# Attention beside an MLP on one core: the main loop's order on five engines from one searched table, with shared PSUM places

## The chip, the core and the metric

The kernel runs on one core of a Trainium2 chip. The core has a matrix engine (PE, with its weight loads shown apart as PEld), a vector engine (DVE), an activation engine (ACT), a general engine (POOL) and an engine that issues most DMAs (SP). The metric is device time in microseconds (us), the median of several runs.

## What is computed

A layer norm of the input is fed to two branches, and all is summed: attention with 32 query heads of 16 columns that share one key and one value head, and a two-layer MLP with the Mish function.

```python
# B, S, D, H, Dh, F = 1, 2048, 512, 32, 16, 1792
xn = layernorm(x)                                   # over D, eps 1e-5
q  = (xn @ wq) as 32 heads of 16;  k, v = xn @ wk, xn @ wv    # [S, 16]
p  = softmax(q @ k.T * Dh ** -0.5)                  # per head, [S, S]
attention = concat(p @ v) @ wo
h   = xn @ w1 + b1
mlp = (h * tanh(softplus(h))) @ w2
out = x + attention + mlp                           # all in float32
```

## The kernel before

**Tiles.** Tokens are cut into 4 chunks `c` of 512; `X[c]` is the transposed, normed chunk as a high and a low part. Weights and activations are split in the same way (`split`: ACT copies the high part, POOL subtracts to get the low part), and a product of two is the sum of three terms. The 32 heads of 4 chunks make 32 units `u` of 4 heads and 512 queries each. A unit needs three passes:

- `s`: scores of queries (rows) against keys, 64 tiles, whose maxima DVE takes straight from PSUM (TENSOR_REDUCE into `nm`). At a unit's end the maxima are negated, transposed by PE (`mt`), split by DVE (`mhl`) and sent by four SP DMAs into rows of the unit's query tile `QS` (`place_maxima`).
- `e`: the scores again, transposed and with the maxima already subtracted, 64 tiles of 128 keys x 512 queries. ACT takes the exponential out of PSUM into a probability slot `pt`.
- `o`: value steps, 16 a unit, each four matmuls (one a head, 32 columns of the array each) that add into one PSUM tile; each shows twice in the trace (4096 rows for 2048 matmuls). ACT reads the tile out (`ov`) after the 16th.

Maxima of unit u+1 run beside exponentials and value steps of unit u. In between stand the products of the MLP and of the output projection, cut into pieces that fill one PSUM tile: `h` (X by w1, 56), `y` (activation by w2 in five parts, 80) and `f` (attention by wo, 12, and four at the very end). Mish goes through ACT (exponential, logarithm, exponential), DVE (a clamp, `tu`) and POOL.

**Lanes and value steps.** Contraction of `s` and `e` needs 64 rows or fewer, and products of 128 rows are cut into two halves. So PE works in lanes: a matmul of 64 rows on the upper half of the array beside another on the lower half. Two neighbours on different halves run at once, and I call that a slot of the lanes; where the next matmul is for the same half, one half stays empty for a slot. Value steps use all 128 rows, and between lanes and value steps PE changes its mode.

**PSUM and slots.** PSUM has eight tiles of 512 columns: three for `s` (`m`), one pair (`e2`) and one single (`e1`) for `e`, one for half products (`misc`), one for `o`. Probabilities lie in three pairs (`WIDE`) and four singles (`SINGLE`), ten heads in all. An exponential is wide (two heads, one ACT instruction of 1024 columns) or single.

**What sets the order.** `PLAN` is a string with one letter for each action: a value step, or a pair of jobs for the two lanes (maximum, wide, single, half or nothing), with or without a drain of PE ahead of it. `commit` carries an action out and lets a class `Clock` with prices for each operation tell when weights, Mish stages and maxima are due (`later`, `run_due`, `flush`). PE, ACT, DVE and POOL then work in the order in which the calls were made; the order of SP's DMAs was set by the framework. Blocks of w1, w2 and wo are split once, stored to DRAM (`w_dram`) and loaded again from there (`block`); `X` has two places, chunks 2 and 3 are stored ahead of the loop and loaded again (`need_x`).

Ahead of the loop stand loading, layer norm, transposes, keys, values, all queries (stored to `q_dram`) and the maxima of unit 0. Behind it stands `last_quotient`: the sum, division and projection of the last unit.

Of the kernel before, what the change touches and what calls it, by code (L numbers as in the profile page):

```python
# [31 lines left out]
FILLS = 3 * (2 * NC * DT * FT + 2 * NC * DT * DT - DT) - 3 * DT * DT  # L32
ACTS, RING, QTS = 7, 6, 3


SLOT, LOAD, DRAIN = 0.228, 0.105, 0.19
VALUES, INTO_VALUES, INTO_LANES = 0.87, 0.1, 0.13
READY, LATE, BACK = 0.43, 0.115, 0.165
REDUCE, EXP1, EXP2 = 0.598, 0.477, 0.904
ADD, POOL_ADD = 0.6, 1.3  # L40
STEP = 3.2
SLACK, OVERDUE = 0.5, 6.0
WEIGHTED = "wq", "w1", "w2", "wo"
WEIGHTS, FIRST = 8.0, 14.0
ATTENDED = 5
WIDE, SINGLE = 3, 4
U_MAX = 16384.0

# [5 lines left out]
JOBS = None, "maximum", "wide", "single", "half"  # L54
ACTIONS = ["values", "place"] + [(a, b, d) for a in JOBS for b in JOBS for d in (False, True)]
LETTERS = ".!" + string.ascii_letters
PLAN = (
    "ssRtisRtssiRQAQSQUQQyQUtwCq.Gww.qow.soo.qsCCsMsRyQUQ.myq.ssCsCsVQOQQSSGQ.myq.ssMsCCsM.myq.wwUQ.QQUSSQQOUQtCq"
    "Cs.mMCCs.sMssCs.qsCRUQQSSQ.GwQSOUQ.GwQS.QQQUSSQOG.QSotsMisCCsMs.qmy.qoCs.GwCRQUQSSQUQ.myG.ssiysMs.yssq.ysssM"
    "iisCCq.mwUS.QQUQOSQ.MsCssiMsiisCq.GQQSOOQUOQSQS.ssMsCCsiiG.ASQQQU.yUQQQ.GCCssisiiG.oAQQOOQOSQUo.Gmy.Mym.qQOQ"  # L60
    "SSG.QSSQtMssCCsMs.yq.sssMCCsiiq.RUQSSQQOOG.MCCssq.qSSQQOG.qym.MssCCsMRQSSQUQ.Gym.qyss.qCCssiq.qCCssiG.GSQSQO"
    "UQOQSQS..qCCssiMsiysMs.CAm.yQQQUOOQSSUQQ..sAsCsisMisy.mqy.QGSQSOQUOQ.GCCssiMsisy.wUw.QQUQyOQUQ.wGSQ.QUQyQOQU"
    ".tssMCCsisq.QQQSUSQOQNsCsCsM.oqo.Gsys.Gym.UQSSQQUQOOQuSG.osMo.MsCCss.qCCss.GQQSSOQOOUQOQy.qmy.MssysiMs.qCCss"
    "iG.QQUSSQQOUQOQy.qwo.MsssCCMs.ossAis.ymG.yQUQQOOSQUo.GssCCisMis.UyQQQ.GSQSQOG.qCCssiMsisy.QUQSSQQU..qwStsiMs"
    "isCCq..qCCssiMsisyq.wSGQ.QUSSQQQ.qsCCsiMsisysM.CAm.yQQQUOOQSSQUQ..oCssMisiCCsq.mAw.UQyQQOUQOOQSUw.qsCo.MssCC"
# [24 lines left out]
    "my.GQSQSOQOUQ.GCCssiMsisy.qmy.UwwQ.QUQSSQQg.CCsMssiisy.GwS.QUSSQQQU.wCMssisiCsA.myQU.QQQUSSQ.GoCsiiMsisCCsM."  # L90
    ".qwwOOOUQOQSSQUQ.mys.qCCssisMiCCsq.mAw.QQUQSSQOUQ.wSUm.oCssMisiCCsq.ssG.GQSSQOQUOQSQS.MssCCsM.mqy.MmCo.qwSQO"
    "OUQQSSG.sssCCMs.qoCs.Gwo.GSSQQOUQOyQG.myq.ymG.oAm.sssMCsCisMisRSQUQS.QQSUQS.sMssCCs.MCCssq.GSSQQOUQOQSSQ..qC"
    "CssiMsisCCq.msA.GQSQOOQUOQSQSG.qCCs.qCCssiG.GSSQQOUQOQSSQ.qmCC.MCmw.USSQQQU.GssCCis.qCsCsMsRSQSQ.Gym.USSQQQU"
    ".qssCCiMsisiis.Ao.GQQSSOG.ysssMiisCCq.mwS.QQUSSQQU.ssMCCssiMsisy.Gw.UQSQQOUQOyQUQ..qCsCsiMsisy.wUQQSOQOUQ.Ms"
    "sCCsiq.GSSQQOUQOQy.qmCC.qwo.qCCssiMsisyG.wQQUS.GQQSSOq.ysssM.MCCssq.AQoQOOUOOSS..CCssMiiiiyg.ASOOOOUOOOy.Mii"
    "CCiMii..TSOOOOUOOy.MiiyiiiM.CCVOOOSSU.yOU.CCiVOOyOOU.AC.Miy.UOOyOOU.ACiiigiiy.My.MCCiig.ASOOOOU.y.MyiiiiMPyO"
    "U.yU.yEOO.."
# [4 lines left out]
def attention_and_mlp(ctx: ExitStack, tc: tile.TileContext, x, wq, wk, wv, wo, w1, b1, w2, out):  # L102
# [3 lines left out]
    ACT, DVE, POOL = Counted(nc.scalar), Counted(nc.vector, ADD), Counted(nc.gpsimd, POOL_ADD)  # L106
# [5 lines left out]
    ps = pool("ps", space=PSUM)  # L112

# [6 lines left out]
    def bank(tag, name, bufs):  # L120
        return ps.tile([P, CT], F32, tag=tag, name=name, bufs=bufs)
# [10 lines left out]
    def mbank(name):  # L132
        return late_ps.tile([P, CT], F32, tag="m", name=name, bufs=3) if late_ps else pair_bank(name)[:, 0]
# [3 lines left out]
    now, queue, forced = [-100], [], [False]  # L137
    read = {"u": 0.0, "n": 0.0}

    def later(delay, stage, tag, at=0.0, step=None):  # L140

        if clock and step is None:
            queue.append((now[0], stage, tag, max(clock.t + STEP * delay, at)))
        else:
            queue.append((now[0] + delay if step is None else step, stage, tag, at))

    def due(e):
        return e[0] <= now[0] and (not clock or e[3] <= clock.t)

    def run_due(n):  # L150
        some = [e for e in queue if e[2][0] != "m" and due(e)]
        if clock and clock.act > clock.t + SLACK:
            some = [e for e in some if e[2][0] in WEIGHTED or e[3] + OVERDUE < clock.t]
        for entry in some[:n]:
            if entry in queue:
                queue.remove(entry)
                entry[1]()

    def flush(*tags):
        was, forced[0] = forced[0], True  # L160
# [5 lines left out]
        forced[0] = was  # L166

    def waits(tag, k, stage):

        if forced[0] or not clock or clock.t >= read[tag] and (tag, k - 1) not in (e[2] for e in queue):  # L170
            return False
        later(0, stage, (tag, k), max(read[tag], clock.t + 0.5))
        return True

    def split(hi, lo, src):

        ACT.activation(hi, src, AF.Copy)
        POOL.tensor_tensor(out=lo, in0=src, in1=hi.bitcast(F32), op=ALU.subtract)


    kept = {}

    stored = {"wblk": [], "w2": []}
# [1062 lines left out]
```

## Time and profile before

| | |
|---|---|
| median of 3 runs | 1688.11 us (1687.91 to 1688.55) |
| profiled execution | span 1686.8 us, and 1688.1 with what lies around it |
| PE busy, matmuls | 1631.5 us, 11549 |
| DVE, ACT, POOL busy | 1367.7, 1334.0, 784.7 us |
| DMA | 149.90 MB, mean 89 GB/s |
| granted PE clock, mean | 0.991 |

Busy time is the time in which an engine has at least one instruction under way. PE's matmuls are pipelined, so that two that overlap count once and a busy PE is not PE at its peak. A row of the timeline gives start, length, engine, line, operation, what is written and read, shapes and count; several instructions of one kind in a row are merged. Lines are those of the kernel before: L383 is `s`, L459 `e`, L476 `o`, L812 a piece's product, L415 the transpose of maxima; L1209 and L1217 are helpers of DVE and ACT through which all reductions and activations pass.

### The profile page before, as it was taken

The numbers are of one execution on the slowest core, as the hardware profiler recorded it, in microseconds if no ns is written. First come the engines' busy times: TensorE is split into PE (matmuls) and PEld (weight loads), VectorE is DVE, ScalarE is ACT, GpSimd is POOL, SyncE is SP. The second block draws the span as 40 slices with busy tenths as digits, with TensorE's granted clock in tenths as the row PEclk, the third lists the DMA queues.
The fourth block names the chain that finished last, engine by engine and source line by source line (L and its number), as shares of the span: only waits on it lengthen the run. The fifth ranks groups of instructions, "written<-read, shape, count | busy, mean of one in ns | idle before, by whom it ended". The sixth has DMA issues, their size and how long they took to land.

```text
span 1686.8 us, 29994 instructions
## 1 busy us (share of the span) xinstructions
PE 1631.5 (97%) x11549; PEld 862.1 (51%) x11549; DVE 1367.7 (81%) x2269; ACT 1334.0 (79%) x1997; POOL 784.7 (47%) x695
## 2 busy tenths in 40 slices
PE   6989999999999999999999999999999999999998
PEld 4554454445554454554555555554555545455554
DVE  7817988878888888888888889888888888998821
ACT  5437888788888888887788888888688888877885
POOL 5734565647275444534072733626053545340532
PEclk9989999999999999999999999999999999999999
DMA  6465103133232211141312221122312311132130
GB/s 209 184 259 190 36 30 129 37 130 111 73 92 74 84 55 64 53 137 66 116 54 91 81 68 50 66 67 73 123 42 83 91 53 63 54 105 78 38 120 26
DMA packets 66821, 149.90 MB, mean 89 GB/s; under 512 B 9430, under 2 KB 19734, under 8 KB 66422
## 3 DMA queue, kind: packets, MB, share of 16 engines
q1 hardware_dynamic: 66614, 147.96, 26.2%
q8 instruction: 91, 1.49, 0.4%
q14 instruction: 52, 0.43, 0.1%
q10 hardware_dynamic: 64, 0.02, 0.0%
HBM read 97.98 MB, written 49.02 MB: 87 GB/s over the span
## 4 chain that ended last, share of the span: by engine, by line
PE 86%; DVE 5%; ACT 3%; DMA 3%; issue 2%; POOL 2%; SPq 0%; ACTq 0%; POOLq 0%; DVEq 0%
PE o L476 29%; PE e L459 17%; PE s L383 14%; PE y L812 11%; PE h L812 11%; DVE nm L1209 3%; PE f L812 3%; DMA q_dram<-q 1%; ACT pt L1217 1%; DMA raw_w<-in_B_w_dram 1%; PE f_last L574 1%; ACT q L1217 1%; PE kv L307 1%; POOL q L1193 1%; PE mt L415 0%
## 5 line engine op out<-in xcount | busy, mean ns | idle before, releaser
L1209 DVE TENSOR_REDUCE nm<-s 128x1 f32<-128x512 f32 (+1 forms) x2016 | 1278.1, 692 | 215.0 <-PE s L383 147.6
L1217 ACT ACTIVATE pt<-e 128x1024 f32<-128x1024 f32 (+1 forms) x1431 | 1048.5, 780 | 244.3 <-PE e L459 162.1
L383 PE MATMUL s<-KS,QS 48*128 48x512 f32 x2048 | 735.3, 432 | 5.3 <-DVE nm L1209 2.7
L459 PE MATMUL e<-QS,KS 64*128 64x512 f32 x2048 | 690.5, 429 | 12.5 <-ACT pt L1217 11.2
L476 PE MATMUL o<-pt,V 128*32 128x512 f32 x4096 | 541.6, 606 | 0.0
L383 PEld LDWEIGHTS s<-KS,QS 48*128 48x128 f32 x2048 | 346.0, 186 | 210.4 <-DVE nm L1209 174.6
L459 PEld LDWEIGHTS e<-QS,KS 64*128 64x128 f32 x2048 | 325.0, 185 | 244.6 <-ACT pt L1217 183.3
L812 PE MATMUL y<-w,act 64*128 64x512 f32 x1344 | 366.9, 401 | 1.5
L812 PE MATMUL h<-X,w 64*128 64x512 f32 (+1 forms) x1320 | 358.7, 403 | 5.2 <-ACT w L1217 3.9
L812 PEld LDWEIGHTS y<-w,act 64*128 64x128 f32 x1344 | 238.8, 185 | 64.9 <-issue 32.2
L812 PEld LDWEIGHTS h<-X,w 64*128 64x128 f32 (+1 forms) x1320 | 237.4, 186 | 55.0 <-issue 21.1
L476 PEld LDWEIGHTS o<-pt,V 128*32 128x32 f32 x4096 | 84.2, 108 | 170.2 <-issue 162.7
L1193 POOL TENSOR_TENSOR tn<-tn,tr 128x512 f32<-128x512 f32 x54 | 69.7, 1290 | 215.2 <-ACT tr L1217 215.2
L1197 POOL TENSOR_SCALAR tn<-tu 128x512 f32<-128x512 f32 x54 | 33.6, 622 | 285.5 <-DVE tu L1205 285.5
L1193 POOL TENSOR_TENSOR y<-y,ty 128x512 f32<-128x512 f32 x80 | 103.7, 1298 | 106.4 <-ACT ty L1217 106.4
L1193 POOL TENSOR_TENSOR act<-th,act 128x512 fp32r<-128x512 f32 x56 | 72.0, 1286 | 53.3 <-ACT act L1217 44.4
L812 PE MATMUL f<-wo,ohl 64*128 64x512 f32 x288 | 76.5, 400 | 2.1 <-DVE yf L1193 1.4
L1193 POOL TENSOR_TENSOR th<-th,tn 128x512 f32<-128x512 f32 x56 | 73.1, 1305 | 0.0
L1193 POOL TENSOR_TENSOR tz<-tz,tn 128x512 f32<-128x512 f32 x54 | 69.9, 1294 | 4.5
L1193 POOL TENSOR_TENSOR th<-th,tz 128x512 f32<-128x512 f32 x54 | 69.8, 1293 | 4.2
L1193 POOL TENSOR_TENSOR tn<-tn,tu 128x512 f32<-128x512 f32 x54 | 69.6, 1289 | 4.5
L1193 POOL TENSOR_TENSOR ohl<-oc,ohl 128x512 fp32r<-128x512 f32 (+1 forms) x16 | 20.8, 1298 | 97.4 <-ACT ohl L1217 65.4
(96 smaller groups left out, 889.6 us busy)
## 6 DMA issues: line engine op xcount, KB each, us to landing
w<-w_dram SPq DMA_DIRECT2D x84, 512.0 KB
w_dram<-w SPq DMA_DIRECT2D x28, 512.0 KB
QS<-q_dram SPq DMA_DIRECT2D x62, 192.0 KB
q_dram<-q SPq DMA_DIRECT2D x16, 512.0 KB
wo<-wo_dram SPq DMA_DIRECT2D x16, 512.0 KB
o_dram<-ov SPq DMA_DIRECT2D x31, 256.0 KB
raw_w<-in_B_w_dram SPq DMA_DIRECT2D x28, 256.0 KB
xs<-in_A_x_dram SPq DMA_DIRECT2D x16, 256.0 KB
```

The lines of the kernel that those rows point to most:

```text
L307: PE.matmul(p, w, x, start=n == 0, stop=n + 1 == len(products))
L383: PE.matmul(tile, QS[u][rows, pair, qt * P : (qt + 1) * P], KS[rows, kc * CT : (kc + 1) * CT], start=True, stop=True,)
L459: PE.matmul(bank, KS[rows, kt * P : (kt + 1) * P], QS[u][rows, pair], start=True, stop=True)
L476: PE.matmul(O[u][h * 32 : (h + 1) * 32], V[:, kt], PT[(u * KT + kt) * HG + h], start=kt == 0, stop=kt == KT - 1,)
L574: PE.matmul(LAST[t], OHL[NC - 1, mt][:, i, t * P : (t + 1) * P], RINGED[NC - 1, "wo", mt][:, j], start=mt == 0 and k == 0, stop=mt == DT - ...
L812: PE.matmul(self.p, w[rows], x[rows], start=self.first, stop=last)
L1193: return self.engine.tensor_tensor(out=out, **kw)
L1197: return self.engine.tensor_scalar(out, *args, **kw)
L1209: return self.engine.tensor_reduce(out=out, in_=in_, **kw)
L1217: return self.engine.activation(out, in_, func, **kw)
```

## The change

The main loop is no longer planned by `Clock` and due times. A longer string `PLAN` is read token by token, and each token calls one thing on one engine: maxima (`s`, `S`: the case gives the lane), single or wide exponentials (`e`, `E`, `f`, `F`), halves of products (`h`, `H`), value steps (`V`), a drain (`|`), the placing of maxima (`P`) and their sending (`D`), a piece's read-out (`Z`), the stages of Mish (`U`, `N`, `M`, `A`), splitting and storing weights (`B`, `K`), their loads (`W`, `G`), query loads (`L`), reloads of X (`X`) and the steps of the attention's division. `PIECES` lists the pieces in order. SP's DMAs stand in the order of the tokens too.

A digit behind a token names one of seven PSUM tiles, any of which takes `s`, `e`, `mt` or a piece; the eighth is for `o`. A letter names one of 16 probability slots. A wide exponential takes two neighbouring tiles. Pieces may be open on both lanes at once. `X[0]` is the one place of X in the loop: chunks 1, 2 and 3 are stored ahead of it and loaded over the one before. The clamp of Mish goes to POOL.

```diff
-JOBS = None, "maximum", "wide", "single", "half"
-ACTIONS = ["values", "place"] + [(a, b, d) for a in JOBS for b in JOBS for d in (False, True)]
+RAWS, BLOCKS, ATTENDED, SLOTS = 3, 3, 5, 16
 PLAN = (
-    "ssRtisRtssiRQAQSQUQQyQUtwCq.Gww.qow.soo.qsCCsMsRyQUQ.myq.ssCsCsVQOQQSSGQ.myq.ssMsCCsM.myq.wwUQ.QQUSSQQOUQtCq"
+    "S6s0S1Bs2s3s4BS5H6GAs0BS1HHHHS2HGs3HHKHBHHH|hhhS0S1s2AhhhGS3hF4aeF0ches2hhE3es4he5fS2S0hKZe1gE4hs3Ve5iE6jf0kWEs2"
...
-        X[c] = pool.tile([P, 2, DT, CT], F32R, tag="X", name=f"X{c}", bufs=2)
+        X[c] = pool.tile([P, 2, DT, CT], F32R, tag="X", name=f"X{c}", bufs=3 if c else 1)
...
-            if i in (8, 14):
-                c = 2 + (i == 14)
+            if i in (8, 12, 16):
+                c = (2, 1, 3)[(i - 8) // 4]
                 flush(("lo", c))
                 spill(c, FLAT[c])
...
-    ctx.enter_context(tc.manual_schedule(engines={E.PE, E.Activation, E.DVE, E.Pool}))
+    ctx.enter_context(tc.manual_schedule(engines={E.PE, E.Activation, E.DVE, E.Pool, E.SP}))
...
+    banks = late_ps.tile([P, 8, CT], F32, name="banks")
+    BANK = [banks[:, i] for i in range(8)]
+    slots = tiles(SLOTS // 2, [P, 2, CT], "pt")
...
+    def exponentials(a, n, wide, word):
+        n = 2 * n + a
+        if waiting:
+            head, bank, slot = waiting.pop()
+            score(n, BANK[bank + 1])
+            PT[head], PT[n] = (slots[slot // 2][:, k] for k in range(2))
+            ACT.activation(slots[slot // 2], banks[:, bank : bank + 2], AF.Exp, scale=SCALE)
+            return
+        bank, slot = word(), word()
+        score(n, BANK[bank])
+        if wide:
+            waiting.append((n, bank, slot))
+            return
+        PT[n] = slots[slot // 2][:, slot % 2]
+        ACT.activation(PT[n], BANK[bank], AF.Exp, scale=SCALE)
+
+    def exponential(k):
+        h, n = TH[k % 3], TN[k % 2]
+        ACT.activation(tu, h, AF.Exp)
+        POOL.tensor_scalar_min(tu, tu, U_MAX)
...
+    def reload(c):
+        X[c] = X[0]
+        SP.dma_start(out=flat(X[0].rearrange("p a t n -> p a (t n)")), in_=x_dram[c])
```

**PE in the middle of the loop** (behind value step 267 of 512 before, 266 after; `s`, `e`, `y`, `mt`, `o` are the passes above; in the new program L504 is `s`, L445 `e`, L865 a piece's half, L508 `o`, and each writes the tile `banks`). Before:

```order
L383 MATMUL s_0_1_0_11896<-KS,QS_71 128x512 [waits DVE_49]
L812 MATMUL y_0_0_11860<-w_11011,act_2_11116 128x512
L459 MATMUL e_11900<-QS_72,KS 128x512 [waits Activation_49]
L812 MATMUL y_0_0_11860<-w_11011,act_2_11116 128x512 [waits Pool_49]
L459 MATMUL e_11900<-QS_72,KS 128x512
L459 MATMUL e_11910<-QS_72,KS 128x512
L383 MATMUL s_1_0_0_11914<-KS,QS_71 128x512 [waits DVE_49]
L383 MATMUL s_2_1_1_11917<-KS,QS_71 128x512 [waits DVE_49]
L415 MATMUL mt_0_11920<-ident,nmr_0_11874 16x128 [waits DVE_49]
L476 MATMUL o_11486<-pt_11868,V 32x512
```

PE after:

```order
L445 MATMUL banks<-KS,QS_78 128x512 [waits DVE_49]
L865 MATMUL banks<-ring_1077,act_1081 128x512 [waits Activation_49]
L445 MATMUL banks<-KS,QS_78 128x512
L865 MATMUL banks<-ring_1077,act_1081 128x512
L504 MATMUL banks<-QS_77,KS 128x512 [waits DVE_49]
L865 MATMUL banks<-ring_1075,act_1086 128x512
L865 MATMUL banks<-ring_1077,act_1081 128x512 [waits Pool_49]
L865 MATMUL banks<-ring_1078,act_1082 128x512
L504 MATMUL banks<-QS_77,KS 128x512 [waits Activation_49]
L865 MATMUL banks<-ring_1078,act_1082 128x512
```

Two pieces are open side by side now (`ring_1075` and `ring_1077`), and a matmul of either pass waits for DVE or ACT, whichever read its tile last, where before `s` waited for DVE and `e` for ACT.

**ACT behind the read-out of unit 15** (`pt` is a probability slot, 512 columns a single exponential, 1024 a wide one). Before:

```order
L1217 ACTIVATE pt_11454<-e_11452 128x512 [waits PE_49]
L1217 ACTIVATE pt_11465<-e_11461 128x1024 [waits PE_49]
L1217 ACTIVATE pt_11480<-e_11478 128x512 [waits PE_49]
L1217 ACTIVATE pt_11493<-e_11491 128x512 [waits PE_49]
L1217 ACTIVATE th_4_11510<-h_4_11351,b1s 128x512 [waits PE_49]
L1217 ACTIVATE pt_11513<-e_11507 128x1024 [waits PE_49]
```

After:

```order
L922 ACTIVATE pt_1071<-banks 128x1024 [waits PE_49]
L930 ACTIVATE pt_1070<-banks 128x512 [waits PE_49]
L930 ACTIVATE pt_1069<-banks 128x512 [waits PE_49,Activation_49]
L930 ACTIVATE pt_1070<-banks 128x512 [waits PE_49,Activation_49]
L930 ACTIVATE pt_1072<-banks 128x512 [waits PE_49] x2
L930 ACTIVATE pt_1073<-banks 128x512 [waits PE_49] x2
```

Most exponentials are single now: over the loop 223 wide and 1602 single ones for 617 and 814.

**SP ahead of the loop** (the stores of a chunk's queries: two thirds and one third of them). Before:

```order
L354 DMA q_3_dram<-q_3_695 128x512 [waits DMAHW7_49,Activation_49]
L980 DMA KS<-ones 2x16x128 [waits DMAHW0_49]
L353 DMA q_3_dram<-q_3_695 128x2x512 [waits DMAHW1_49,Pool_49]
L354 DMA q_0_dram<-q_0_748 128x512 [waits DMAHW2_49,Activation_49]
L353 DMA q_0_dram<-q_0_748 128x2x512 [waits DMAHW3_49,Pool_49]
```

After:

```order
L413 DMA q_3_dram<-q_3_705 128x2x512 [waits DMAHW0_49,Activation_49,Pool_49]
L414 DMA q_3_dram<-q_3_705 128x512 [waits DMAHW1_49]
L250 DMA raw_w_747<-in_B_w_dram 128x4x128 [waits DMAHW2_49]
L413 DMA q_0_dram<-q_0_758 128x2x512 [waits DMAHW4_49,Activation_49,Pool_49]
L414 DMA q_0_dram<-q_0_758 128x512 [waits DMAHW7_49]
```

The store that needs ACT alone went ahead of the one that needs POOL; now it stands behind it.

More of the change, by code (lines that the diff above doesn't have):

```diff
@@ L105, in attention_and_mlp @@
     PE, SP = nc.tensor, nc.sync
-    ACT, DVE, POOL = Counted(nc.scalar), Counted(nc.vector, ADD), Counted(nc.gpsimd, POOL_ADD)
+    ACT, DVE, POOL = nc.scalar, nc.vector, nc.gpsimd
     def pool(name, bufs=1, **kw):
@@ L132, in mbank, with later @@
     def mbank(name):
[L133 to L148, printed above, removed]
+        return pair_bank(name)[:, 0]
+    now, queue = [-100], []
+    def later(delay, stage, tag, step=None):
+        queue.append((now[0] + delay if step is None else step, stage, tag))
     def run_due(n):
-        some = [e for e in queue if e[2][0] != "m" and due(e)]
-        if clock and clock.act > clock.t + SLACK:
-            some = [e for e in some if e[2][0] in WEIGHTED or e[3] + OVERDUE < clock.t]
+        some = [e for e in queue if e[2][0] != "m" and e[0] <= now[0]]
         for entry in some[:n]:
@@ L165, in flush @@
                     entry[1]()
[L166 to L173, printed above, removed]
     def split(hi, lo, src):
@@ new lines, in divide, with attention @@
+    def divide(j):
+        rows = rows_of(j)
+        o, d, r, z = oc[rows], dc[rows], r0[rows], z0[rows]
+        ACT.activation(r, z, AF.Exp, scale=-1.0)
+        POOL.tensor_tensor(out=d, in0=d, in1=r, op=ALU.mult)
+        POOL.tensor_scalar(d, d, -1.0, 2.0, op0=ALU.mult, op1=ALU.add)
+        POOL.tensor_tensor(out=r, in0=d, in1=r, op=ALU.mult)
+        POOL.tensor_tensor(out=o, in0=o, in1=r, op=ALU.mult)
+    def attention(j):
+        rows = rows_of(j)
+        OHL[divmod(j, DT)] = t = OHLS[j % ATTENDED]
+        split(t[rows, 0], t[rows, 1], oc[rows])
@@ L664, in act @@
-        def act():
-            if not late_pool or k >= used[0] + ACTS:
-                return later(1, act, ("h", k))
-            A[c, f] = late_pool.tile([P, 2, CT], F32R, tag="act", name=f"act{c}_{f}", bufs=ACTS)
-            split(A[c, f][:, 0], A[c, f][:, 1], h)
-        later(max(1, 8 + k - 100 - now[0]), exponential, ("u", k))
-        if f + 1 == FT and c + 2 < NC:
-            need_x(c + 2)
-    Y, YD = {}, {}
-    RINGED = {}
-    ring, groups = [], []
-    spent, begun_finals, ended_finals = [0], [0], [0]
@@ L994, in attention_and_mlp @@
         place_maxima(0, slice(1, 2))
-        for c in range(2, NC):
-            del X[c]
     late_pool, late_ps = pool("late"), pool("late_ps", space=PSUM)
-    total = NU * KT
-    maxima_of = [[(u, step, pair) for u in range(1, NU) for step in range(KT) for pair in range(2)] for _ in range(2)]
-    reduced_of = [0] * NU
-    clock = POOL.clock = Clock()
-    placed = clock.placed
-    for b in there:
-        there[b] = 0.0
-    def one_maximum(a, n):
-        u, step, pair = maxima_of[a][n]
-        maxima(u, step, pair, a)
-        reduced_of[u] += 1
-        if reduced_of[u] == HG * KT:
-            negate_maxima(u)
-            later(0, lambda: place(u), ("m", u), clock.dve + 0.5)
@@ L1017, in place @@
-    def place(u):
-        place_maxima(u)
-        free, _ = clock.m.pop(0)
-        clock.t = max(clock.t, free) + 2 * SLOT
-        clock.dve = max(clock.dve, clock.t + READY)
-        clock.m.append((clock.dve + 0.6, clock.n))
-    def one_half(a):
-        done[0] += 0.5
-        ready[0].last = clock.n
-        if ready[0].half(a):
-            ready.pop(0)
-            more()
-    def more():
-        while len(ready) < 3 and ask():
-            pass
-        clock.pieces = [p.state() for p in ready[:2]]
@@ new lines, in half, with maximum @@
+    def half(lane, bank):
+        p = next((p for p in opened if p.todo[lane]), None)
+        if p is None:
+            p = todo.pop(0)
+            opened.append(p)
+            p.begin(BANK[bank()])
+        p.half(lane)
+        if not any(p.todo):
+            opened.remove(p)
+            ended.append(p)
+    waiting, reduced = [], [0] * NU
+    def maximum(a, n, bank):
+        u, r = divmod(n, 2 * KT)
+        maxima(u + 1, r // 2, r % 2, a, bank)
+        reduced[u + 1] += 1
+        if reduced[u + 1] == HG * KT:
+            negate_maxima(u + 1)
@@ new lines, in attention_and_mlp @@
+    for token in word:
+        k = count.get(token, 0)
+        count[token] = k + 1
+        if token in "sS":
+            maximum("sS".index(token), k, BANK[digit()])
+        elif token in "eEfF":
+            a = "eE".index(token) if token in "eE" else "fF".index(token)
+            n = count.get(("e", a), 0)
+            count["e", a] = n + 1
+            exponentials(a, n, token in "fF", digit)
+        elif token in "hH":
+            half("hH".index(token), digit)
+        elif token == "|":
+            PE.drain()
+        elif token == "V":
+            values(*divmod(k, KT))
+        elif token == "P":
+            sent[0] = place_maxima(k, bank=BANK[digit()])
+        elif token == "D":
+            sent[0]()
+        elif token == "Z":
+            ended.pop(0).end()
+        elif token == "U":
+            exponential(k)
+        elif token == "N":
+            ACT.activation(tz, TN[k % 2], AF.Ln, bias=2.0)
+        elif token == "M":
+            inverse(k)
+        elif token == "A":
+            hidden_tile(k)
+        elif token == "B":
+            split_block()
+        elif token == "K":
+            store_block()
+        elif token == "W":
+            request("w1", k % FT, WB[k % BLOCKS])
+        elif token == "G":
+            request(*blocks[k], RG[k % RING])
+        elif token == "L":
+            LOADS[k]()
+        elif token == "X":
+            reload(k)
+        elif token == "J":
+            SP.dma_start(**dict(zip(("out", "in_"), outgoing.pop(0))))
+        else:
+            {"O": attended, "C": collect, "Q": logarithm, "R": divide, "T": attention}[token](k)
```

884 lines of the change are left out of this document (340 added, 544 removed), and 7 rows, old and new, of the table PIECES.

## The prediction

> **What bounds the kernel now.** I read the page first, then busy time by stretch, then the instructions of PE in order of time.
>
> ```profile
> PE 1631.5 (97%) x11549; PEld 862.1 (51%) x11549; DVE 1367.7 (81%) x2269; ACT 1334.0 (79%) x1997; POOL 784.7 (47%) x695
> ...
> PE 86%; DVE 5%; ACT 3%; DMA 3%; issue 2%; POOL 2%; SPq 0%; ACTq 0%; POOLq 0%; DVEq 0%
> ```
>
> PE is 97% busy and holds 86% of the chain that ended last, but its matmuls overlap, so that share doesn't say how close the order on PE is to its floor. DVE and ACT are close behind. The next table (start:end, length, then busy time and count per engine, granted clock, DMA share, GB/s) cuts the span at the first and last row of the main loop's matmuls, quoted below it.
>
> ```profile
> 0.00:118.00 118.00, 92.00 (x413) 65.28 (x414) 69.63 (x115) 54.53 (x99) 71.16 (x72) 0.97 0.62 216
> 118.00:1668.00 1550.00, 1525.43 (x11084) 787.53 (x11084) 1292.29 (x2143) 1276.71 (x1891) 712.24 (x623) 0.99 0.24 80
> ```
> ```profile
> 117.66 0.79 PE L812 MATMUL h<-X,w 64*128 64x512 f32 x1 [3.92 <-ACT w L1217]
> ...
> 1666.55 2.06 PE L476 MATMUL o<-pt,V 128*32 128x512 f32 x16
> ```
>
> The loop runs from 117.7 to 1666.55 + 2.06 = 1668.6: 1550.9 us. In it PE has two states: lanes (two 64-row matmuls side by side, one per half of the array: `s`, `e`, and the halves `h`, `y`, `f`), and value steps (`o`, all four heads). Its timeline prices both.
>
> ```profile
> 1079.46 1.07 PE L476 MATMUL o<-pt,V 128*32 128x512 f32 x8
> ...
> 1080.46 0.50 PE L383 MATMUL s<-KS,QS 48*128 48x512 f32 x1
> 1080.79 0.39 PE L459 MATMUL e<-QS,KS 64*128 64x512 f32 x1
> ...
> 1081.03 0.39 PE L459 MATMUL e<-QS,KS 64*128 64x512 f32 x1
> ...
> 1081.26 0.39 PE L383 MATMUL s<-KS,QS 48*128 48x512 f32 x1
> ```
>
> Start to start, a slot of the lanes is 0.23 (1081.03, 1081.26). After a value step the first slot comes 1.00 later, and the second 0.33 after that. What an unpaired half, a drain and a second value step in a row cost:
>
> ```profile
> 717.33 0.39 PE L812 MATMUL h<-X,w 64*128 64x512 f32 x1
> 717.37 0.50 PE L383 MATMUL s<-KS,QS 48*128 48x512 f32 x1
> 717.56 0.39 PE L812 MATMUL h<-X,w 64*128 64x512 f32 x1
> 717.88 1.06 PE L476 MATMUL o<-pt,V 128*32 128x512 f32 x8
> 719.06 0.49 PE L812 MATMUL h<-X,w 64*128 64x512 f32 x1
> ```
> ```profile
> 885.19 0.39 PE L383 MATMUL s<-KS,QS 48*128 48x512 f32 x1
> 885.69 0.18 PEld L812 LDWEIGHTS y<-w,act 64*128 64x128 f32 x1 [0.54 <-issue]
> ...
> 886.03 0.39 PE L812 MATMUL y<-w,act 64*128 64x512 f32 x1
> ```
> ```profile
> 802.24 0.28 PE L415 MATMUL mt<-ident,nmr 128*16 128x128 f32 x1
> ...
> 802.45 1.92 PE L476 MATMUL o<-pt,V 128*32 128x512 f32 x16
> ...
> 804.30 0.50 PE L459 MATMUL e<-QS,KS 64*128 64x512 f32 x1
> ```
>
> The `h` at 717.56 has no partner and still takes a slot; `o` follows 0.32 after it. 717.88 to 719.06 has a drain in it: 1.18 for 1.00, so a drain behind a value step costs 0.18. A drain among lanes (885.19 to 885.69 to 886.03) costs 0.50 + 0.34 - 2 x 0.23 = 0.38. Two value steps in a row take 1.85 (802.45 to 804.30): the second adds 0.85.
>
> So a run of lanes with n slots between two value steps takes 1.00 + 0.33 + 0.32 + (n - 2) x 0.23 = 1.19 + 0.23 n. The table before has 3710 slots (460 of them with one half empty), 484 runs of value steps with 28 further steps in them, and 46 drains (40 among lanes, 6 behind values): 853.3 + 484 x 1.19 + 28 x 0.85 + 40 x 0.38 + 6 x 0.18 = 853.3 + 576.0 + 23.8 + 15.2 + 1.1 = 1469.4. The loop took 1550.9, so 81.5 is left over. About 5 of it is the loop's first 10 us, whose granted clock is 0.52:
>
> ```profile
> 118.00:128.00 10.00, 9.49 (x37) 5.43 (x35) 7.54 (x12) 1.54 (x3) 1.26 (x2) 0.52 0.63 211
> ```
>
> About 9 is the 31 transposes of the maxima (an estimate: 802.24 to 802.45 above, and about 0.1 more ahead of it than ahead of `o`). Some 67 is PE waiting for a PSUM place to be read out:
>
> ```profile
> PEld e L459 <- ACT pt L1217: 183.3, 305, 4.9
> PEld s L383 <- DVE nm L1209: 174.6, 239, 1.7
> ```
>
> (total us, times, longest). These two contain the normal idle time behind each value step, so they bound the 67 from above and show who is waited for.
>
> **The change, part by part.** *Fewer slots.* The new table, read through with the same rule (neighbours on different halves share a slot), gives 3584 slots for the same 6960 matmuls: 126 x 0.23 = 29.0 off PE's path. Nothing hides it: PE is the chain. *Runs and drains.* 469 runs with 43 further steps, 50 drains (46 behind values, 4 among lanes): 558.1 + 36.6 + 8.3 + 1.5 = 604.5, for 616.1 before: 11.6 off. Together 40.6.
>
> *Seven shared places.* Before, `e` has one pair and one single, `s` three, a half piece one. A place claimed again sooner than matmul (0.39), read-out (0.60, 1.02 or 0.68 by the next rows but one) and about 0.1 of signalling is a wait that is written into the order. Laid on the rows' prices, 352 of 3410 claims before are too early, by some 30 in sum; now 192 of 4182, by some 6. Scaled by count the 67 become 37, by size 14; between these lies 25, which I take, since engines that run behind add what the order doesn't show: 42 off. Bounds: 0 left (67 off), and all 67 left, if sharing only moves the wait. Sixteen probability slots for ten let `e` run further ahead of the value steps; but `o` comes 0.32 behind the last slot at 717.88 and doesn't wait there for its exponentials, so I count nothing more.
>
> *ACT.* 617 wide exponentials (two heads) and 814 single ones become 223 and 1602.
>
> ```profile
> L1209 DVE TENSOR_REDUCE nm<-s 128x1 f32<-128x512 f32 x1984 | 1240.1, 684 | 207.1 <-PE s L383 139.7 <-PE e L459 36.3 <-PE y L812 12.6
> ...
> L1217 ACT ACTIVATE pt<-e 128x1024 f32<-128x1024 f32 x617 | 631.2, 1023 | 87.3 <-PE e L459 69.0 <-PE h L812 6.1 <-PE y L812 3.3
> L1217 ACT ACTIVATE pt<-e 128x512 f32<-128x512 f32 x814 | 485.2, 596 | 156.9 <-PE e L459 93.1 <-PE s L383 32.6 <-DMA y<-in_A_x_dram 8.8
> ```
> ```profile
> 127.57 0.91 ACT pt L1217
> ...
> 129.00 0.49 ACT pt L1217
> ```
>
> Back to back (the chain's rows) a wide one holds ACT 0.91 and a single one 0.49, so 394 wide into 788 single is 788 x 0.49 - 394 x 0.91 = 27.6 more. ACT is busy 1276.7 of 1550; with 28 more in a loop of some 1470 that is 89%. It is off the chain while PE has other places to write to; cost taken 0, and what it costs if that fails is the second rival. The Trainium skill, Perfetto Trace Analysis, § Optimizing Scalar/DVE Operations, says that such instructions carry a fixed overhead, so larger ones help an engine that is saturated, and that splitting them helps where the engine is not saturated but makes bubbles on others. The rows agree on the overhead (0.07 a split); by its first half the time would be that of the second rival, by its second half the forecast.
>
> *DVE and POOL.* The 54 clamps move from DVE to POOL.
>
> ```profile
> L1205 DVE TENSOR_SCALAR tu<-tu 128x512 f32<-128x512 f32 x54 | 33.1, 613 | 0.0
> L1197 POOL TENSOR_SCALAR tn<-tu 128x512 f32<-128x512 f32 x54 | 33.6, 622 | 285.5 <-DVE tu L1205 285.5
> ```
>
> DVE loses 33.1 of its 1292.3, and no reduction stands behind a clamp that waits for ACT; POOL gains about 54 x 0.62 = 33 on 712 of 1550 and has idle time for it. I count 0 here: the gain is in the 42.
>
> *One chunk of X, and SP's queue.* Three reloads of 2 MB for two, each into the place of the chunk just used, so it can start only behind that chunk's last `h`.
>
> ```profile
> 738.00:742.00 4.00, 4.00 (x32) 2.02 (x32) 3.37 (x7) 3.85 (x7) 3.84 (x5) 1.00 0.96 408
> ```
>
> In this stretch, right behind the issue of a reload before, DMA moves 408 GB/s: 2 MB take about 5 us. In the new order at least 93 slots of other work stand between the last `h` of a chunk and the first of the next, 21 us in lanes alone: hidden, 0; uncovered, and twice as slow, 3 x 10 = 30. SP's DMAs now stand in the table's order, so a DMA that waits holds up the ones behind it. That was so before as well:
>
> ```profile
> SPq L423 <- DVE mhl L1193: 243.2, 22, 34.2
> ```
>
> SP stood up to 34 us at one row of maxima, and PE's waits name no DMA of any size. Cost 0; upper bound with the third rival.
>
> *Ahead of the loop.* Its last third is a chain of queries: ACT, POOL, store, and the buffer again.
>
> ```profile
> 103.76 1.31 POOL q L1193
> 105.08 2.88 DMA q_dram<-q
> 108.07 0.61 ACT q L1217
> ```
> ```profile
> 112.95 0.32 SPq L354 DMA_DIRECT2D q_dram<-q  x1
> ...
> 114.35 0.37 SPq L353 DMA_DIRECT2D q_dram<-q  x1
> ```
>
> Before, one of the two stores (L354) goes out ahead of POOL's part; now both go out behind it, L354's second. That adds 0.32 to each link, 6 links: +2. A spill of chunk 1 (4 x 512 KB) is new there; DMA is 62% busy. Bounds -2 (one block split less just before the loop) to +8. The end, 18 us of fixed chain behind the last `o`, keeps its instructions: 0.
>
> Sum against the profiled execution (span 1686.8, run 1688.1 with what lies around it, which is the median of the three runs): 1688.1 - 40.6 - 42 + 2 = 1607.5, so **1608**, 4.7% less.
>
> **Rivals.** *Only the slots pay.* The shared places are held longer because ACT has more to do, and the 67 stay: 1688.1 - 40.6 + 2 = 1649.5. For it: ACT waits for PE and PE for ACT in turn (`e` 183.3 above). Against it: the claims lie further apart, and DVE, the other reader, gets lighter.
>
> *ACT becomes the bound; slower.* If ACT can't be busy more than the 1276.7 / 1550 = 82.4% it is now, because its idle time comes from the order in which it must take what PE gives, its 27.6 cost 27.6 / 0.824 = 33.5 and PE's savings are spent waiting for it: 1688.1 + 33.5 = 1721.6. Against it:
>
> ```profile
> ACT pt L1217 <- PE e L459: 162.1, 301, 1.9
> ```
>
> 162 us of ACT's idle time is waiting for `e`, which a faster PE shortens. It decides once ACT needs over 95% of the loop; I get 89%.
>
> *Data come late.* A reload, a weight block or a row of maxima stands on SP behind a DMA that waits; 31 units x 1 us plus two uncovered reloads of 10 is 51, on top of the forecast: 1660. It would turn slower only from 79 / 31 = 2.5 us in every unit. Against it is SP's row above.
>
> **How the numbers follow.** Forecast 0.66, only the slots 0.17, late data 0.08, ACT 0.09. The range takes the forecast's bounds (no bank wait left: 1582.5; all: 1649.5) and reaches to the late data: 1583 to 1660, which leaves out ACT and the far ends, some 0.15 to 0.2. A measurement of this kernel tells 0.2% (3.4 us) from no change. Faster: forecast, slots and late data, less a little for their tails, 0.88; slower 0.09; the same 0.03.
>
> **What would show it.** In the new trace: from the first lane matmul to the last `o` about 1470; 469 separate runs of `o`; slots still 0.23; idle time of `e`'s and `s`'s weight loads before ACT and DVE clearly below 183 and 175; 223 wide and 1602 single exponentials; ACT near 89% of the loop; no wait of PE for X or QS over some us; the loop starting at about 119 to 120. Wrong would be a loop near 1510 (waits moved, not gone), ACT over 95%, or waits of PE for DMAs in each unit.

## The result, and the profile after

| | before | after |
|---|---|---|
| median of 4 runs | 1688.33 us | 1616.42 us (1615.51 to 1617.15) |
| profiled execution, span | 1686.8 us | 1615.4 us |
| ahead of the loop | 117.7 us | 123.7 us |
| main loop | 1550.9 us | 1474.6 us |
| behind the last `o` | 18.2 us | 17.0 us |

The ratio is 0.957 (95% interval 0.956 to 0.959): 4.3% faster, 72 us, where 4.7% and 80.6 us were forecast. First a correction to what was told ahead: in the paragraph before the rows of PE the two line numbers of the new program are exchanged. L445 is `s` (it reads KS and QS, 48 rows), L504 is `e` (QS and KS, 64 rows).

The page of the kernel after, busy time and shares of the chain that ended last:

```profile
PE 1573.9 (97%) x11549; PEld 850.3 (53%) x11549; DVE 1348.3 (83%) x2215; ACT 1342.7 (83%) x2391; POOL 862.5 (53%) x749
...
PE 88%; POOL 4%; DMA 3%; ACT 2%; DVE 1%; issue 1%; SPq 0%; ACTq 0%; POOLq 0%; DVEq 0%
```

As before, PE's share says nothing about the gain: 97% both times. The loop's two ends in PE's timeline, and its stretch in the table by windows (start:end, length, busy and count of PE, PEld, DVE, ACT, POOL, then the granted clock, DMA share, GB/s):

```profile
123.74 1.20 PE L445 MATMUL banks<-KS,QS 48*128 48x512 f32 x7 [3.13 <-ACT q L403]
...
1595.57 2.78 PE L508 MATMUL banks<-pt,V 128*32 128x512 f32 x24
```
```profile
124.00:1598.00 1474.00, 1463.32 (x11087) 773.33 (x11085) 1272.66 (x2090) 1286.48 (x2287) 790.76 (x678) 0.99 0.26 85
```

The loop is 1595.57 + 2.78 - 123.74 = 1474.6 us. ACT is busy 1286.5 of it, 87%. The waits of PE's weight loads for the readers of PSUM (total us, times, longest):

```profile
PEld banks L445 <- DVE nm L457: 84.1, 105, 0.8
PEld banks L504 <- DVE nm L457: 82.4, 103, 0.8
PEld banks L445 <- ACT pt L930: 53.2, 96, 1.4
PEld banks L504 <- ACT pt L930: 49.9, 80, 1.7
PEld banks L504 <- ACT pt L922: 14.2, 21, 0.8
```

Before, `e` waited 183.3 for ACT and `s` 174.6 for DVE. Now each waits for both, since the place that it takes may have had either reader, and the five rows add up to 283.8 for 357.9. None of these rows names a DMA. The groups of exponentials:

```profile
L930 ACT ACTIVATE pt<-banks 128x512 f32<-128x512 f32 x1602 | 862.7, 605 | 125.8 <-PE banks L504 73.3 <-PE banks L445 35.3 <-PE banks L865 7.5
L922 ACT ACTIVATE pt<-banks 128x1024 f32<-128x1024 f32 x223 | 227.5, 1027 | 43.2 <-PE banks L504 34.5 <-PE banks L445 6.3 <-PE banks L865 0.8
```

A slot is what it was, 0.23 from one L865 to the next:

```profile
1078.81 0.39 PE L865 MATMUL banks<-X,wblk 64*128 64x512 f32 x1
...
1079.04 0.39 PE L865 MATMUL banks<-X,wblk 64*128 64x512 f32 x1
```

Put to the prices of the prediction (0.23 a slot, 1.19 a run, and so on), the new table's loop (counted in the table, as before) costs 3584 x 0.23 + 469 x 1.19 + 43 x 0.85 + 4 x 0.38 + 46 x 0.18 = 1428.8, so 45.8 us of the 1474.6 are left over; before, 81.5 were. The loop's 76.3 us are then 40.6 of fewer slots, runs and drains, and 35.7 of less waiting. That is a sum on paper, and the second number is what the first leaves over; the experiments test each half.

### The profile page after: what moved, and what is told of

The parts are those of the page before. It is cut to its first block, busy times and chain, and to the rows that moved or that the text cites. A ratio compares the mean times of both kernels' runs of the same rounds, so it can differ in the third digit from the quotient of the medians.

```text
span 1615.4 us, 30289 instructions
## 1 busy us (share of the span) xinstructions
PE 1573.9 (97%) x11549; PEld 850.3 (53%) x11549; DVE 1348.3 (83%) x2215; ACT 1342.7 (83%) x2391; POOL 862.5 (53%) x749
## 3 DMA queue, kind: packets, MB, share of 16 engines
q8 instruction: 91, 1.49, 0.4%
## 4 chain that ended last, share of the span: by engine, by line
PE 88%; POOL 4%; DMA 3%; ACT 2%; DVE 1%; issue 1%; SPq 0%; ACTq 0%; POOLq 0%; DVEq 0%
PE banks L508 30%; PE banks L865 24%; PE banks L504 16%; PE banks L445 16%; DMA q_dram<-q 2%; DMA x_dram<-X 1%; POOL tn L937 1%; POOL tu L935 1%; PE banks L590 1%; ACT pt L930 1%; PE kv L367 1%; PE xt L330 1%; POOL q L407 0%; PE q L651 0%; PE banks L476 0%
## 5 line engine op out<-in xcount | busy, mean ns | idle before, releaser
L457 DVE TENSOR_REDUCE nm<-banks 128x1 f32<-128x512 f32 x1984 | 1245.4, 684 | 158.1 <-PE banks L445 110.7
L930 ACT ACTIVATE pt<-banks 128x512 f32<-128x512 f32 x1602 | 862.7, 605 | 125.8 <-PE banks L504 73.3
L445 PE MATMUL banks<-KS,QS 48*128 48x512 f32 x1984 | 687.7, 423 | 4.5 <-ACT q L403 3.1
L504 PE MATMUL banks<-QS,KS 64*128 64x512 f32 x2048 | 683.7, 420 | 0.8 <-ACT ty L875 0.4
L508 PE MATMUL banks<-pt,V 128*32 128x512 f32 x4096 | 537.6, 604 | 0.0
L445 PEld LDWEIGHTS banks<-KS,QS 48*128 48x128 f32 x1984 | 328.4, 185 | 195.8 <-DVE nm L457 84.1
L504 PEld LDWEIGHTS banks<-QS,KS 64*128 64x128 f32 x2048 | 328.7, 185 | 194.8 <-DVE nm L457 82.4
L865 PE MATMUL banks<-X,wblk 64*128 64x512 f32 x1296 | 344.1, 403 | 5.2 <-ACT wblk L233 1.9
L865 PE MATMUL banks<-ring,act 64*128 64x512 f32 x1344 | 339.2, 398 | 2.9
L922 ACT ACTIVATE pt<-banks 128x1024 f32<-128x1024 f32 x223 | 227.5, 1027 | 43.2 <-PE banks L504 34.5
L865 PEld LDWEIGHTS banks<-X,wblk 64*128 64x128 f32 x1296 | 216.5, 187 | 60.8 <-issue 37.2
L865 PEld LDWEIGHTS banks<-ring,act 64*128 64x128 f32 x1344 | 214.1, 185 | 57.1 <-issue 33.1
L508 PEld LDWEIGHTS banks<-pt,V 128*32 128x32 f32 x4096 | 85.4, 108 | 172.4 <-issue 161.0
L935 POOL TENSOR_SCALAR tu<-tu 128x512 f32<-128x512 f32 x54 | 80.4, 1489 | 164.2 <-ACT tu L934 164.1
L865 PE MATMUL banks<-ring,ohl 64*128 64x512 f32 x288 | 66.7, 396 | 0.2
```

What stands on the lines that cost most here:

```text
L445: PE.matmul(tile, QS[u][rows, pair, qt * P : (qt + 1) * P], KS[rows, kc * CT : (kc + 1) * CT], start=True, stop=True,)
L457: DVE.tensor_reduce(out=m[:, a : a + 1], in_=tile, axis=AX.X, op=ALU.max)
L504: PE.matmul(bank, KS[rows, kt * P : (kt + 1) * P], QS[u][rows, pair], start=True, stop=True)
L508: PE.matmul(BANK[7][h * 32 : (h + 1) * 32], V[:, kt], PT.pop((u * KT + kt) * HG + h), start=kt == 0, stop=kt == KT - 1,)
L865: PE.matmul(self.p, w[rows], x[rows], start=self.first, stop=not any(self.todo))
L922: ACT.activation(slots[slot // 2], banks[:, bank : bank + 2], AF.Exp, scale=SCALE)
```

## The experiments

Each edit is made to the changed kernel (1616.4, loop 1474.6) unless the text says "before". "Loop" is read from the trace of each run as above.

**1 and 2. The clamps back on DVE.**

```diff
         ACT.activation(tu, h, AF.Exp)
-        POOL.tensor_scalar_min(tu, tu, U_MAX)
+        DVE.tensor_scalar_min(tu, tu, U_MAX)
```

> The changed kernel (1616.4) with the 54 clamps of Mish back on DVE, right behind ACT's exponential in the order; POOL loses 54 x 1.49 us. Theory as predicted (slots and waits for places carry the gain, the clamp's move is worth 0): 1616 +- 2. Rival (DVE's queue is nearly full in the new order, and a clamp that waits for ACT holds up the maxima behind it, so that PE waits for its places): about 1635, with more idle time of PE's weight loads before DVE; the 54 clamps are then worth up to 54 x 0.4 to 0.6 = 22 to 33 us.

Measured: 1638.5 us (ratio to before 0.9708, 0.9693 to 0.9722), loop 1497.1, so 22 us slower. The groups of the clamp in the kernel after and in this run, and PE's waits for DVE in this run:

```profile
L935 POOL TENSOR_SCALAR tu<-tu 128x512 f32<-128x512 f32 x54 | 80.4, 1489 | 164.2 <-ACT tu L934 164.1
```
```profile
L935 DVE TENSOR_SCALAR tu<-tu 128x512 f32<-128x512 f32 x54 | 30.5, 564 | 15.3 <-ACT tu L934 15.1
```
```profile
PEld banks L445 <- DVE nm L457: 96.7, 131, 1.7
PEld banks L504 <- DVE nm L457: 89.6, 129, 1.4
```

The clamps hold DVE 30.5 us, and it stands idle 15.3 ahead of them. PE's two waits for DVE rise from 166.5 to 186.3: 19.8 of the loop's 22.5. Is it the time or the standing still?

```diff
         ACT.activation(tu, h, AF.Exp)
-        POOL.tensor_scalar_min(tu, tu, U_MAX)
+        clamps.append([4, n])      # carried out on DVE behind the fourth maximum from here
```

The two POOL operations behind the clamp move with it. (In one of the 54 tiles the logarithm then runs ahead of the clamp, at 525.9 us for 527.2, and takes an older value, so only this kernel's time is of use.)

> As the run before, but the clamp is called on DVE four maxima later, when ACT's exponential is long done, so that DVE doesn't stand still for it. If the move is worth 0: 1616 +- 2. If the clamp only costs when it holds up the maxima while it waits for ACT: back near 1616 to 1620. If DVE's time itself is short (54 x 0.42 on DVE's queue): about 1630 to 1635, as in the run before.

Measured: 1638.7 us (0.9708, 0.9692 to 0.9724), loop 1498.0. The clamp's group (busy, mean, then idle time ahead of it) and a new wait of ACT:

```profile
L938 DVE TENSOR_SCALAR tu<-tu 128x512 f32<-128x512 f32 x54 | 33.3, 617 | 0.0
```
```profile
ACT tz L996 <- POOL tn L940: 12.5, 9, 3.0
```

DVE no longer waits for ACT at the clamp, and the time is the same, so the loss doesn't need that wait; in this order the clamps' move is not worth 0. The split is not clean: POOL's two operations moved too, and ACT now stands 12.5 us for them at its logarithm, for 1.4 in run 1. At the price of load on ACT in run 7 (55%) those 11 us are 6 of the loop's 23.4. That most of the rest is DVE's own time is the likeliest reading.

**3. 114 slots more.**

```diff
+        if u and (2 * step + pair) % 16 == 8:
+            score_tiles(u, qt, kc, pair, {a: tile})
         m = score_tiles(u, qt, kc, pair, {a: tile})
```

> The changed kernel with 124 of the 1984 maxima's matmuls issued twice (same operands, same tile), evenly over the loop: 114 more slots of the lanes. Theory (a slot is 0.23 us of PE's path and nothing hides it): 114 x 0.23 = 26 us more, 1642. Rival (PE waits for its readers anyhow, so added slots fill waits): under half of it, below 1629.

Measured: 1638.6 us (0.9708, 0.9694 to 0.9723), loop 1496.4: 21.8 us for 114 slots, 0.19 each for 0.23. The other 17% seems to go into waits that were there: PE's two waits for single exponentials fall from 53.2 and 49.9 to 49.9 and 46.5. An added slot is on the path, as the theory has it.

**4. The places no longer shared, in the new order.** The digits of the table are replaced: maxima and transposes take tiles 0 and 1, exponentials 2 and 3, pieces 4 to 6; the order of the tokens stays, with four drains added.

> The changed kernel's order with the seven places no longer shared: two for maxima (and their transposes), two for exponentials (one pair), three for pieces, each the one free longest; four drains added where the order of a piece's halves needs them. Theory (in this order the sharing keeps PE from waiting): the claims that come too early go from some 190 to over 1200, laid out at the rows' prices some 550 us more, 2170. Rival (only the order counts, the sharing little): below 1650.

Measured: 2330 us (1.381, 1.377 to 1.384), loop 2194. PE's waits:

```profile
PEld banks L445 <- DVE nm L457: 398.0, 625, 1.9
PEld banks L504 <- ACT pt L930: 350.3, 596, 1.7
PEld banks L504 <- ACT pt L922: 175.6, 153, 1.9
```

This order can't do with two, two and three places of its own. No other division was tried, and no order was laid out afresh for fixed places. The estimate was 2170. It made no allowance for PE's granted clock, 0.938 over this run and 0.988 after. In stretches of 10 us, the length times the share of the clock that is missing adds up to 138 us in this loop and to 10 in that of the kernel after, so the clock can be at most 128 of the 160 us beyond the estimate.

**5 and 9. The other way round: sharing in the old order.** A list of digits, one for each claim, gives the kernel before seven places for all; its order on PE is untouched.

```diff
-        return late_ps.tile([P, CT], F32, tag="m", name=name, bufs=3) if late_ps else pair_bank(name)[:, 0]
+        return place_for() if late_ps else pair_bank(name)[:, 0]
...
-            e = late_ps.tile([P, k, CT], F32, tag=f"e{k}", name=f"e{n}", bufs=1)
+            e = place_for(k) if k == 2 else place_for()[:, None]
```

> The kernel before (1688) in its own order, with seven places that anyone may take (each claim takes the one read out longest ago, from a list; five drains added where a piece's halves need them). Theory as predicted (sharing itself spares 42 us of waits): about 1646. Rival (in the old order the waits come from the order and the readers, and sharing does nothing by itself): -6 to 0 by laying the order out at the rows' prices, 1682 to 1690.

Measured: 6346 us (3.76). The build was at fault, not the idea. Six of the places were cut from one tile of six, and halves of pieces wait 763 times for DVE's maxima and 568 times for ACT's exponentials, for 9 and 3 times in the run below. My list also handed out places that were claimed and not yet read; how much each of the two costs is not shown. Rows of its timeline:

```profile
3000.41 0.60 ACT L1266 ACTIVATE pt<-banks 128x512 f32<-128x512 f32 x1 [4.48 <-PE banks L507]
3001.06 0.28 PEld L859 LDWEIGHTS banks<-w,act 64*128 64x128 f32 x1 [1.20 <-ACT pt L1266]
3001.06 0.79 PE L859 MATMUL banks<-w,act 64*128 64x512 f32 x1 [0.69 <-ACT pt L1266]
```

A half of a piece (L859) starts 0.05 behind the end of an exponential, which it doesn't read. The run says nothing on the theory. It was made again with all places cut from one tile of eight and a list that keeps a place until its reader is through:

> The kernel before (1688) in its own order with seven shared places, now cut from one tile of all eight banks, and with 45 drains more where a piece's halves need them (by the prediction's rows 45 x 0.18 to 0.38 = 8 to 17 us). Theory as predicted (sharing itself spares 42 us of waits): 1688 - 42 + 13 = 1659. Rival (sharing does nothing by itself in an order that wasn't made for it): 1688 + 8 to 17, and up to 12 more where the place that is free longest is the wrong one: 1696 to 1717.

Measured: 1731.1 us (1.026, 1.025 to 1.028), loop 1596.9, 46 us longer than before. Its waits, L429 being `s` and L505 `e`:

```profile
PEld banks L429 <- DVE nm L1256: 116.0, 153, 1.7
PEld banks L505 <- DVE nm L1256: 105.9, 145, 2.2
PEld banks L505 <- ACT pt L1264: 99.9, 171, 5.4
```

By the prediction's rows at most 17 of the 46 are drains, and the clock's part, counted as in run 4, is some 8 (20 for 12 before). With this list, sharing in an order made for fixed places spares nothing and costs. Whether a better list would bring it to 0 stays open; the theory's 1659 is 72 us away.

**6. The clamps on POOL in the old order.**

```diff
-            DVE.tensor_scalar_min(u, u, U_MAX)
+            (POOL if late_pool else DVE).tensor_scalar_min(u, u, U_MAX)
```

> The kernel before (1688) with the 54 clamps of the loop on POOL, nothing else. After the changed kernel lost 22 us when its clamps went back to DVE: if DVE's time is short in either order, 1688 - 20 = 1668. If only the new order is that tight (the old one leaves DVE idle in front of each clamp), 1688 +- 2.

Measured: 1686.8 us (0.9993, 0.9983 to 1.0002), loop 1549.6. No effect: taking 33 us off DVE is worth nothing there, while putting them back costs 22 in the new order. POOL takes 80.4 us for them, and in the loop PE waits for POOL once, for 0.8 us.

**7. About as much load on ACT as the prediction saw added.**

```diff
+        if n % 32 == 8 and n - 2 in PT:
+            ACT.activation(PT[n - 2], PT[n - 2], AF.Copy)
```

> The changed kernel (1616.4) with 43 copies of 128 x 512 (a probability slot onto itself, right after it was written) added on ACT, some 0.55 us each, 24 us in all: about the load that the change added there. Theory as predicted (ACT is off the chain): below 1621. Rival (every engine of the new order is that tight, as DVE was): 17 to 27 more, 1633 to 1643.

```profile
L930 ACT ACTIVATE pt<-pt 128x512 f32<-128x512 f32 x43 | 27.4, 637 | 0.7
```

Measured: 1630.6 us (0.9663, 0.9647 to 0.9679), loop 1489.8: 27.4 us of copies cost 15.2, 55%. That is between the two theories: ACT is 87% busy, and load on it is still not free.

**8 and 10. The chain of queries ahead of the loop.** The chain of waits of the kernel after, one link:

```profile
111.93 1.30 POOL q L407
113.24 0.36 SPq L413
...
113.65 3.02 DMA q_dram<-q
...
116.82 0.61 ACT q L403
...
117.45 0.64 ACT q L404
```

111.93 to 118.22 (the chain's next POOL row) is 6.29. A link is two queries and not one: there are two buffers, and another query's POOL row, which is not on the chain, lies in between.

```profile
111.93 1.29 POOL L407 TENSOR_TENSOR q<-q 128x512 fp32r<-128x512 f32 x1 [2.16 <-ACT q L404]
114.71 1.30 POOL L407 TENSOR_TENSOR q<-q 128x512 fp32r<-128x512 f32 x1 [1.50 <-ACT q L404]
118.22 1.29 POOL L407 TENSOR_TENSOR q<-q 128x512 fp32r<-128x512 f32 x1 [2.20 <-ACT q L404]
```

So a query takes 3.14, and where the two expectations below speak of 6.3 and 5.65 a query, they mean a link. Both edits exchange the two stores, the first also gives four buffers:

```diff
-        q = first.tile([P, 2, CT], F32R, tag="q", name=f"q{c}_{mt}", bufs=2)
+        q = first.tile([P, 2, CT], F32R, tag="q", name=f"q{c}_{mt}", bufs=4)
...
-                        SP.dma_start(out=d[:2].rearrange("k p n -> p k n"), in_=qf)
                         SP.dma_start(out=d[2], in_=qf[:, 0])
+                        SP.dma_start(out=d[:2].rearrange("k p n -> p k n"), in_=qf)
```

> The changed kernel with the store that doesn't need POOL's part issued first and four buffers for the split queries instead of two. If the +6 at the loop's start is the chain ACT, POOL, store, buffer (6.3 us a query, 5.65 before): the chain goes, a query costs about 2.6 (1.24 on ACT, 1.3 on POOL), and the loop starts 10 to 18 us sooner: 1598 to 1606. If something else sets the start (maxima of unit 0, DMA): 1614 to 1616.

Measured: 1602.9 us (0.9496, 0.9481 to 0.9510), loop start 110.5, loop 1474.1. The store is gone from the chain:

```profile
82.14 19.21 PE q L651 x83
...
104.15 0.61 ACT q L403
104.78 0.64 ACT q L404
105.55 1.30 POOL q L407
106.87 0.61 ACT q L403
```

A query now takes 2.72 (104.15 to 106.87) for 3.14, about the time of its matmuls on PE: 83 in 19.21 are 0.23 each, and a query has twelve. Of the 13.2 us, about 7 are these shorter queries; the rest is that the stretch starts earlier (POOL's first two queries in a row at 83.1 for 89.5).

> The changed kernel (1616.4) with only the order of the two stores of a split query exchanged, so that the one that doesn't need POOL's part goes out first; two buffers as before. If that order makes the loop start late (6.3 against 5.65 us a query over some 6 queries): 1612 to 1614. If the spill of a chunk of X and the late start of the chain do: 1616 +- 1.

Measured: 1611.9 us (0.9553, 0.9538 to 0.9569), loop start 117.5, loop 1474.7. The exchange alone takes back the 6 us: the loop starts 6.2 sooner in the profiled execution, while the medians differ by 4.5. The interval overlaps that of the changed kernel (0.9558 to 0.9585), and the loop's start in the trace tells them apart.

**11. Load off ACT**, on top of run 8.

```diff
+    def pool_split(hi, lo, src):
+        POOL.tensor_scalar(hi, src, 1.0, 0.0, op0=ALU.mult, op1=ALU.add)
+        POOL.tensor_tensor(out=lo, in0=src, in1=hi.bitcast(F32), op=ALU.subtract)
...
-        split(t[:, 0], t[:, 1], TH[k % 3])
+        pool_split(t[:, 0], t[:, 1], TH[k % 3])
```

> The kernel of the run with four buffers (1602.9) with the high parts of the 54 activation tiles copied on POOL (a multiply-add of 0.62 us) instead of ACT: 54 x 0.63 = 34 us off ACT. If load taken off ACT counts as load put on it did (14 us for 24): 1583 to 1590. If the order on PE is now at its floor there and the tightness works one way only: 1600 to 1603.

Measured: 1601.9 us (0.9496, 0.9482 to 0.9511), loop 1473.8. ACT's busy time falls from 1342.4 to 1317.3, and the time is that of run 8. Runs 8 and 11 beat both kernels, by 13 to 15 us and about 85 us.

**12. SP's order left to the framework.**

```diff
-    ctx.enter_context(tc.manual_schedule(engines={E.PE, E.Activation, E.DVE, E.Pool, E.SP}))
+    ctx.enter_context(tc.manual_schedule(engines={E.PE, E.Activation, E.DVE, E.Pool}))
```

> The changed kernel (1616.4) with SP's order left to the framework as before, not to the table. Theory as predicted (a waiting DMA on SP holds up nothing that is needed soon): 1616 +- 2. Rival (SP's stand-still behind rows of maxima, 549 us in the trace, makes loads late): 1600 to 1611.

Measured: 1611.5 us (0.9555, 0.9539 to 0.9571). The trace splits it: the loop starts at 112.3, 11.5 sooner, and is 4.4 longer (1479.0). SP's longest stand, after and here:

```profile
SPq L484 <- DVE mhl L342: 549.3, 30, 31.7
```
```profile
SPq L484 <- DVE mhl L342: 273.4, 26, 31.7
```

The time lies at the edge of the rival's range, but not for its reason: the table's order on SP costs ahead of the loop and not in it, for all of its 549 us.

## Why the prediction was right, and where it was not

The forecast came out 9 us low: the profiled execution is 71.4 shorter for 80.6. The loop's start is 4.1 of it, the loop 6.3, and the end gives back 1.2.

- **Slots, runs and drains, -40.6.** The mechanism holds for a slot added, which costs PE's path 0.19 (run 3). If a slot taken away is worth as much, which no run tried, the 126 are 24 and not 29. What a run of value steps is worth was not tried.
- **Shared places, -42.** The sum leaves 35.7 for this term, so it was mis-sized little, but its reason is half right. "Seven shared places" spare nothing by themselves: the loop of run 9 lost 46 us with them. Without them, in the one division tried, the new order loses 720 (run 4). They are a condition of the order, and the gain belongs to the order that was laid out on them. Which of the order's properties brings the claims apart was only counted (192 early ones for 352), not shown by a run. That the size came out is in part luck: 22.5 of the 35.7 hang on the clamps (next item), which the count of early claims doesn't contain. The 67 us of waits were also too many: the prediction put 5 us to a low clock, for the loop's first 10 us alone, and over the whole loop the count of run 4 gives 12 before and 10 after. With the 9 for the transposes, some 60 us of waits fell to 26.
- **The clamp, 0.** The prediction gave it no price of its own; its gain was to lie in the 42, since "no reduction stands behind a clamp that waits for ACT" any more. The gain does lie there, but it is larger than that reason: run 2 keeps the clamps from waiting and loses as much (with the new wait of ACT named there). With the clamps on DVE the loop keeps 53.8 of its 76.3, in an order laid out without them there; an order laid out with them was not tried. The price on POOL was wrong too, 1.49 each for the 0.62 of another operation, and lies off the path.
- **ACT, 0.** Busy 87%, forecast 89%: the rival that it becomes the bound is out. Its busy time in the loop rose by 9.8, from 1276.7 to 1286.5, and not by 27.6. But load on it is not free: 27.4 us more cost 15.2 (run 7), and PE's waits for single exponentials go from 53.2 and 49.9 to

```profile
PEld banks L445 <- ACT pt L932: 60.7, 116, 1.3
PEld banks L504 <- ACT pt L932: 58.0, 104, 0.8
```

  (L932 is L930, two lines further down). The Trainium skill, Perfetto Trace Analysis, § Optimizing Scalar/DVE Operations, says that larger operations can help where an engine is saturated, and that breaking instructions up may help where it is not but causes bubbles on others. Run 7 shows such bubbles, load on ACT that turns up as waits of PE; whether the split helped is not shown, since no run undid it alone.
- **X and SP, 0.** No wait of PE for X shows. SP's order is not free: +11.5 ahead of the loop and -4.4 in it.
- **Ahead of the loop, +2.** It was 6.1, inside the bounds of -2 to +8. A link was priced at 0.32 more, for the store's issue; it grew from 5.65 to 6.29, 0.64. That is 3 us over the last ten queries. The stretch also starts 6.4 later (POOL's first two queries in a row at 89.5 for 83.1), which the prediction didn't see; in the chain after, a store of X and then a store of queries stand ahead of that:

```profile
61.72 10.62 DMA x_dram<-X
72.36 9.30 DMA q_dram<-q
```

  Of these 9 us the loop's start shows 6.1: before, it stood 2.6 behind POOL's last query, and now 0.8 ahead of it. The exchange of two lines takes 6.2 back (run 10).

What the prediction didn't see is how the pieces hang together. Load is worth nothing where it is taken off (DVE in run 6, in the old order, and ACT in run 11; both times POOL takes it over), and 55% to 83% of its length where it is added to the new order (15.2 of 27.4 on ACT, 22.5 of 30.5 on DVE, 21.8 of 26.2 on PE). My reading is that an order fixed on every engine can't use time that is given back, while any delay in it goes on to PE; that is argued from these runs, and no single one shows it by itself.

## What to carry to other kernels

In an order that is written out for all engines, price an operation added to a busy engine at half its length or more, as it was here, though the engine shows 13% idle time and is hardly on the chain; and don't count on a gain from taking one out while the order stays as it is. A shared pool of buffers is no gain by itself: try it with the old order and the new order without it before you credit it. Look at the part ahead of a long loop with the same care: two exchanged lines and two more buffers were worth another 13 us, as much as a fifth of the whole change.

## What the runs showed of the hardware

- The minimum with a constant took 1.49 us on POOL for 128x512 (L935 after), 0.56 on DVE (L935 in run 1); the multiply-add of the same shape takes POOL 0.62.
- PE's granted clock differed widely between these kernels. In run 5 PE was busy 64% of the span, and the slices of the page (tenths of full clock) read

```profile
PEclk8555555555555555555555555555555555555555
```

  with 0.519 in the mean. With PE busy 86% (run 4) the mean was 0.938, and with 97% (after) 0.988. Even there the first 10 us of the loop had 0.58, right behind PE's idle time of 3.13 at the loop's start:

```profile
124.00:134.00 10.00, 7.99 (x27) 5.22 (x26) 6.76 (x11) 3.91 (x7) 7.11 (x6) 0.58 0.84 303
```

  That PE's waiting is what lowers the clock is a reading of these figures; no run changed the waiting alone.
